# Reordering the first stage, the weight loads and the second product's first units of a fused attention and snake kernel

## The chip, the cores and the metric

The kernel runs on one core of a Trainium2 chip. The metric is the device time of one execution in microseconds (us). The kernel before takes 442.25 us (median of 3 runs, 441.99 to 442.3). The profile names these engines: TensorE (PE in the profile; its weight loads are PEld), VectorE (DVE), ScalarE (ACT), GpSimd (POOL), SyncE (SP, which only issues transfers) and the sixteen DMA engines. A profiled run gives a trace with the start of every instruction. Its span is a little shorter than the device time: 440.3 us in a run of 442.11. The record also has a mean granted TensorE clock for every run, profiled or not.

## The reference

Two things follow each other: attention with normalised q and k, then a two-layer product with the "snake" activation between the layers. Cut to what matters:

```python
# q, k, v: (8 batches, 12 heads, 448 tokens, 64)
rmsnorm = lambda x, g: x / np.sqrt(np.mean(x * x, -1, keepdims=True) + 1e-6) * g
scores = rmsnorm(q, g_q) @ rmsnorm(k, g_k).transpose(0, 1, 3, 2) / 8
attn = softmax(scores) @ v                       # softmax over the last axis
x = attn.transpose(0, 2, 1, 3).reshape(3584, 768)
h = x @ w_in                                     # w_in: 768 x 2048
g = h + np.sin(alpha * h) ** 2 / (alpha + 1e-9)  # snake
out = g @ w_out                                  # w_out: 2048 x 768
```

## The kernel before

The kernel works batch by batch. The first product of batch b is called h(b); the second product is called out(b) here. After h(b) TensorE works on out(b) and on the attention of batch b+1, mixed by a fixed plan, until h(b+1). The stage before h(0) has only attention in it: that is the first stage.

Heads come in pairs, and two head pairs are a *chunk* of q and k: chunks 0, 1 and 2 are batch 0, chunks 3, 4 and 5 batch 1, and so on. What the prediction calls the fifth chunk is chunk 4. Each chunk goes through seven steps: squares of q and of k, q times g, two reduces, root and scaling, transposition.

```python
st.steps = (lambda: square(0), lambda: square(1), fold_g, lambda: reduce(0), lambda: reduce(1),
            lambda: (rsqrt(), scale(0), scale(1)),
            lambda: (transpose(), load_qk(ci + 3) if ci + 3 < NC * B else None))
# transpose(): two DMA transposes on SyncE's queue; load_qk: q and k of a later chunk, on the same queue
# chunks 0 to 2 are transposed by TensorE instead, and VectorE scales them
```

The beginning of the first stage, and its end:

```python
BUSY = (20, 8)                                 # dummy products that keep TensorE busy
c0.square(1), c0.square(0)                     # ScalarE
c0.reduce(1), c0.reduce(0)                     # VectorE
c0.rsqrt(slice(1, 2)), c0.rsqrt(slice(0, 1))   # ScalarE: the two roots
keep_busy(BUSY[0], blank)
spread_g()          # GpSimd g_q*g_k, TensorE spreads it over the partitions, ScalarE copies it
keep_busy(BUSY[1], blank)
c0.fold_g()         # GpSimd: q times g
...
S_(), S_(), S_()    # a score tile (TensorE) and its exponential (ScalarE); S_(n): n dummies in it
c1.rsqrt()
S_(3)
c2.square(0), c2.square(1)     # ScalarE
...
S_()
v_parts[2](), v_parts[3]()
load_w_out(1)                  # second half of w_out, GpSimd's queue
A_(), A_()                     # values of the last two pairs, each 28 matmuls
step_of(NC + 1, 5, 6)()        # chunk 4: scaling (GpSimd), transposes, load of chunk 7
first_product(0, beside_h(0))
```

Out(0) was made in six units of 16 matmuls, each with its own eviction (VectorE copies PSUM to a buffer, which is stored from there).

## Time and profile before

| what | before |
|---|---|
| device time, median (range) | 442.25 us (441.99 to 442.3) |
| TensorE busy | 425.9 us, 97% of the span |
| first exponential / h(0) starts | 14.60 / 44.41 us |
| h(0) to h(1), and each later stretch | 50.36 us |
| half clock | 14.69 to 28.34 us |
| end of ScalarE's last work for h(0) (the last sine and its square), after the start of h's last matmul | 64.55 us, 2.15 us after |

The table is read from the timelines of TensorE and ScalarE. A program with TensorE 97% busy can only get shorter where TensorE waits or runs slowly, and both happen only in the first 95 us. The prediction shows the waits, chain and clock for it. Two more lines will be needed later. One is the issue of chunk 4's transposes in SyncE's timeline (start us, us, engine and line, operation, how many), and the other the end of ScalarE's work for h(0): the table load for the exponentials, which follows the last sine and its square ("the last sine" from here on).

```profile
51.11 14.27 SPq L254 DMA_TRANSPOSE qkT<-qkn  x2
```

```profile
64.57 1.28 ACT L504 ACT_TABLE_LOAD   x1
```

The transposes that were issued from 51.11 us on landed at 70.48 and 71.31 us (read, like all landings of transposes here, from the last semaphore increment of each in the trace). TensorE did not wait for them, since it was not there earlier.

### The profile page before, as it was taken

The numbers are of one execution on the slowest core, as the hardware profiler recorded it, in microseconds if no ns is written. First come the engines' busy times: TensorE is split into PE (matmuls) and PEld (weight loads), VectorE is DVE, ScalarE is ACT, GpSimd is POOL, SyncE is SP. The second block draws the span as 40 slices with busy tenths as digits, with TensorE's granted clock in tenths as the row PEclk, the third lists the DMA queues.
The fourth block names the chain that finished last, engine by engine and source line by source line (L and its number), as shares of the span: only waits on it lengthen the run. The fifth ranks groups of instructions, "written<-read, shape, count | busy, mean of one in ns | idle before, by whom it ended". The sixth has DMA issues, their size and how long they took to land.

```text
span 440.3 us, 9454 instructions
## 1 busy us (share of the span) xinstructions
PE 425.9 (97%) x3811; PEld 220.4 (50%) x3811; DVE 228.1 (52%) x331; ACT 340.1 (77%) x531; POOL 278.0 (63%) x262
## 2 busy tenths in 40 slices
PE   7788999899999999999999999999999999999996
PEld 3234544455555554555555555555555555555563
DVE  3576573456544564464645464545645474246611
ACT  4879888878888788887878788887878788788600
POOL 3867978937698287947599196965599285002300
PEclk9679999999999999999999999999999999999999
DMA  7899999592066803596064902598054900420022
GB/s 251 179 237 251 196 220 226 140 227 78 2 197 180 189 2 76 151 221 120 2 198 146 222 2 51 151 207 159 2 162 116 124 0 18 97 56 1 1 71 73
DMA packets 69296, 55.09 MB, mean 125 GB/s; under 512 B 41460, under 2 KB 65796, under 8 KB 69252
## 3 DMA queue, kind: packets, MB, share of 16 engines
q1 hardware_dynamic: 56690, 40.97, 37.2%
q0 software_dynamic: 11616, 11.81, 17.2%
q10 hardware_dynamic: 946, 1.70, 1.0%
q8 instruction: 30, 0.49, 0.5%
q14 instruction: 14, 0.11, 0.1%
HBM read 45.62 MB, written 11.01 MB: 129 GB/s over the span
## 4 chain that ended last, share of the span: by engine, by line
PE 85%; ACT 4%; POOL 3%; issue 2%; DVE 2%; DMA 2%; SPq 0%; POOLq 0%; DVEq 0%
PE hps L344 33%; PE ops L389 32%; PE av L308 12%; PE sc L292 8%; ACT expT L295 3%; POOL sq L220 2%; DMA g_rows<-in_g_q_dram 1%; POOL qk L223 1%; DMA out_dram<-osb 1%; DVE qkn L245 1%; POOL qkn L245 1%; DVE ms L226 0%; ACT rec L311 0%; PE tp L267 0%; DVE g_sb L331 0%
## 5 line engine op out<-in xcount | busy, mean ns | idle before, releaser
L295 ACT ACTIVATE expT<-sc 128x896 bf16<-128x896 f32 x168 | 145.0, 913 | 33.5 <-PE sc L292 32.2
L389 PE MATMUL ops<-w_out_sb,g_sb 128*128 128x384 bf16 x896 | 156.8, 327 | 0.8 <-DVE osb L395 0.7
L344 PE MATMUL hps<-xT,w_in_sb 128*128 128x448 bf16 x768 | 146.7, 353 | 0.0
L326 POOL TENSOR_TENSOR s<-s 128x448 f32<-128x448 f32 x64 | 59.2, 930 | 101.8 <-ACT s L323 91.0
L389 PEld LDWEIGHTS <-g_sb 128*128 128x128 bf16 x896 | 83.1, 98 | 70.9 <-issue 19.5
L331 DVE SCALAR_TENSOR_TENSOR g_sb<-s,inv_alpha_sb,hps 128x448 bf16<-128x448 f32 x128 | 80.7, 678 | 63.1 <-POOL s L326 63.1
L344 PEld LDWEIGHTS <-w_in_sb 128*128 128x128 bf16 x768 | 74.5, 98 | 71.5 <-issue 2.9
L323 ACT ACTIVATE s<-hps,alpha_sb 128x448 f32<-128x448 f32 x128 | 74.5, 627 | 28.0 <-PE hps L344 26.2
L245 POOL TENSOR_TENSOR qkn<-qk,inv 128x448 bf16<-128x448 f32 x84 | 76.1, 937 | 21.8 <-ACT inv L236 21.3
L317 DVE TENSOR_TENSOR xT<-av,rec 64x448 bf16<-64x448 f32 x96 | 59.7, 622 | 52.9 <-ACT rec L312 33.8
L220 POOL TENSOR_TENSOR sq<-qk 128x896 f32<-128x896 f32 x42 | 69.9, 1678 | 6.1 <-DVE ms L226 4.7
L308 PE MATMUL av<-expT,vb 64*64 64x448 bf16 x672 | 70.4, 353 | 1.2 <-ACT expT L295 1.1
L308 PE MATMUL av<-expT,ones 64*64 64x448 bf16 x672 | 70.4, 353 | 0.0
L226 DVE TENSOR_REDUCE ms<-sq 128x14 f32<-128x896 f32 x42 | 45.3, 1083 | 27.5 <-POOL sq L220 27.2
L292 PE MATMUL sc<-qkT 64*64 64x448 bf16 x672 | 52.1, 369 | 2.7 <-DVE qkT L274 1.1
L395 DVE COPY osb<-ops 128x768 f32<-128x768 f32 (+1 forms) x35 | 27.9, 797 | 50.0 <-PE ops L389 44.1
L223 POOL TENSOR_TENSOR qk<-qk,gg 128x896 f32<-128x896 f32 x24 | 50.1, 2088 | 4.9 <-ACT gg L171 3.3
L308 PEld LDWEIGHTS <-vb 64*64 64x64 bf16 x672 | 37.8, 108 | 15.4 <-issue 3.3
L308 PEld LDWEIGHTS <-ones 64*64 64x64 bf16 x672 | 37.3, 108 | 10.8
L328 ACT ACTIVATE s<-s 128x448 f32<-128x448 f32 x64 | 36.9, 577 | 2.9
L292 PEld LDWEIGHTS <-qkT 64*64 64x64 bf16 x672 | 15.1, 106 | 30.6 <-issue 25.8
L311 ACT ACTIVATE rec<-av 128x448 f32<-128x448 f32 x48 | 26.2, 546 | 3.6 <-PE av L308 3.1
(43 smaller groups left out, 138.9 us busy)
## 6 DMA issues: line engine op xcount, KB each, us to landing
qk<-in_q_dram SPq DMA_DIRECT2D x24, 448.0 KB, 4.9
qk<-in_k_dram SPq DMA_DIRECT2D x22, 448.0 KB, 5.4
out_dram<-osb SPq DMA_DIRECT2D x39, 192.0 KB, 2.9
vb<-in_v_dram POOLq DMA_DIRECT2D x32, 168.0 KB, 6.6
w_in_sb<-in_moe_w_in_dram POOLq DMA_DIRECT2D x2, 1536.0 KB, 20.0
w_out_sb<-in_moe_w_out_dram POOLq DMA_DIRECT2D x2, 1536.0 KB, 27.5
out_dram<-osb SPq DMA_DIRECT2D x26, 96.0 KB, 5.8
qk<-in_k_dram ACTq DMA_DIRECT2D x2, 448.0 KB, 6.0
```

The source lines that it names most:

```text
L220: nc.gpsimd.tensor_mul(st.sq[w], qk[ci][:, w], qk[ci][:, w])
L223: eng.tensor_mul(qk[ci][:, 0], qk[ci][:, 0], gg.to_broadcast([P, 2 * NJ, D]))
L245: eng.tensor_mul(n[:, :, hi, :], x[:, hi], inv[:, hi].unsqueeze(2).to_broadcast([P, NJ, D]))
L292: nc.tensor.matmul(sc[key_rows(pp, hi), pp, :S], qkt[r, 1, j * REST:(j + 1) * REST], qkt[r, 0, :], start=True, stop=True)
L295: nc.scalar.activation(expT[c, j], sc[:, :, :S], ACT.Exp, scale=SCALE)
L308: nc.tensor.matmul(av[o, part, :S], ones[r, :] if part else vb[b][r, hp, j, :], expT[pi // 2, j][r, pi % 2, :], start=(j == 0), stop=(j == ...
L317: nc.vector.tensor_mul(xT[b][r, hp, :], av[r, 0, :S], rec[o, :])
L323: nc.scalar.activation(s1, hps, ACT.Sin, scale=alpha_sb[:, m, :])
L326: nc.gpsimd.tensor_mul(s2, s1, s1)
L331: nc.vector.scalar_tensor_tensor(g_sb[:, m, (b % 2) * S:(b % 2 + 1) * S], s2, inv_alpha_sb[:, m, :], hps, op0=ALU.mult, op1=ALU.add)
L344: nc.tensor.matmul(ps[:, m % 2, :S], w_in_sb[:, kt, m * P:(m + 1) * P], x[:, kt, :], start=(kt == 0), stop=(kt == KT - 1))
L389: nc.tensor.matmul(st["ps"][:, k, :HALF], lhsT, w_out_sb[:, m, half * HALF:(half + 1) * HALF], start=(m == 0), stop=(m == MT - 1))
```

## The change

Its intent is to start the exponentials sooner, to take work off ScalarE's path, to bring w_in in halves so that it does not compete with chunk 4's q and k, to move chunk 4's scaling from before h(0) to beside it, and to evict out(0) in fewer, larger units. The core of it, cut:

```diff
-    BUSY = (20, 8)
+    BUSY = (11, 15)
...
-    w_in_sb = wpool.tile([P, KT, D_FF], BF16)
+    w_in_sb = [wpool.tile([P, KT, D_FF // 2], BF16, name=f"w_in_{half}") for half in range(2)]
...
         def square(w):
-            if early:
+            if ci < 2:                         # chunk 2's squares go to GpSimd
...
-        if m % 2 == 0:
+        if m % 2 == 0 and (b or m <= MT // 2): # three squares of h(0) go to ScalarE
             nc.gpsimd.tensor_mul(s2, s1, s1)
...
-        units = [(i, (0, 1)) for i in order] if b else [(i, (h,)) for h in range(2) for i in order]
+        units = [[(i, half) for half in range(2)] for i in order]
+        if b == 0:                             # four units of out(0): 32, 16, 32 and 16 matmuls
+            units = [[(i, half) for i in rows_] for half in range(2) for rows_ in (order[:2], order[2:])]
...
-    c0.rsqrt(slice(1, 2)), c0.rsqrt(slice(0, 1))
     keep_busy(BUSY[0], blank)
     spread_g()
+    c0.rsqrt(slice(1, 2)), c0.rsqrt(slice(0, 1))
     keep_busy(BUSY[1], blank)
...
-    S_(), S_(), S_()
+    S_(), S_()
     c1.rsqrt()
     S_(3)
-    c2.square(0), c2.square(1)
...
-    S_(2), S_(1), S_()
+    S_(3), S_(2), S_(2), S_(1)
...
+    nc.gpsimd.tensor_copy(gate, qk[NC + 1][:, 1, 0, 0:1])   # wait for chunk 4's k
+    load_w_in(1)
+    load_w_out(0)
...
+    load_w_out(1)
...
-    A_(), A_()
-    step_of(NC + 1, 5, 6)()
-    first_product(0, beside_h(0))
+    S_(), A_(2)            # the last two pairs together, their last tile last
+    c4.rsqrt()
+    beside = beside_h(0)
+    for i, task in ((2, c4.fold_g), (4, lambda: c4.scale(0)), (5, lambda: c4.scale(1)), (6, step_of(NC + 1, 6))):
+        beside.setdefault(i, []).append(task)
+    first_product(0, beside)
```

In every stretch between two h's, the one after h(0) included, three reduces of later chunks also come one slot of the plan later, and beside every h one product of q with g moves to the middle. The two roots of chunk 0 no longer share their PSUM banks. No experiment takes these small moves back alone.

## The prediction

> **What bounds the kernel now.** I read the summary first (TensorE busy 97% of the span), then the start times of the first product h of each of the eight batches, TensorE's waits, the chain in order of time up to 45 us, and the rows of ScalarE, GpSimd and VectorE in that stretch. In TensorE's timeline the h of the eight batches start at 44.41, 94.77, 145.12, 195.48, 245.83, 296.18, 346.54 and 396.89 us: from the first on, one batch every 50.36 us. The waits of TensorE after 40 us are only these (columns: waiting line, releaser, us in total, times, longest):
>
> ```profile
> PE av L308 <- ACT expT L295: 1.1, 2, 0.7
> PE sc L292 <- DVE osb L395: 1.0, 1, 1.0
> PE ops L389 <- DVE osb L395: 0.7, 1, 0.7
> ```
>
> So there is nothing to gain after the second h, and the first 44.4 us plus the stretch from h(0) to h(1) are all that the change can move. In the first stage the chain, in order of time, is (start, us, what):
>
> ```profile
> 1.28 4.28 DMA g_rows<-in_g_q_dram
> ...
> 9.61 2.09 POOL qk L223
> 11.70 0.02 issue
> 11.72 1.16 DVE qkn L245 x2
> ...
> 12.93 0.49 PE tp L267 x14
> ...
> 14.60 2.54 ACT expT L295 x3
> ...
> 42.77 1.71 PE av L308 x32
> 44.48 18.28 PE hps L344 x96
> ```
>
> The reader sees a latency chain up to the first exponential at 14.60 us: g arrives, GpSimd multiplies q by g (9.61 to 11.70), VectorE scales, TensorE transposes. From there ScalarE's program order rules, until the values of the last pair. ScalarE's rows (start, busy us, row, idle before) show what it spends and where it waits:
>
> ```profile
> 9.33 0.21 ACT L171 COPY gg<-gps 128x64 f32<-128x64 f32 x1
> ...
> 18.39 1.78 ACT L217 ACTIVATE g_sb<-qk 128x896 f32<-128x896 f32 x2
> 20.07 2.52 ACT L295 ACTIVATE expT<-sc 128x896 bf16<-128x896 f32 x3
> 24.34 0.92 ACT L295 ACTIVATE expT<-sc 128x896 bf16<-128x896 f32 x1 [1.74 <-PE sc L292]
> ...
> 28.80 0.54 ACT L311 ACTIVATE rec<-av 128x448 f32<-128x448 f32 x1 [0.99 <-PE av L308]
> ```
>
> From the first exponential (14.60) to the end of the last (42.72) are 28.1 us: 21 exponentials at 0.83 (three take 2.54) 17.4, four reciprocal pairs at 1.06 (28.80 to 29.86) 4.2, three pairs for the norm at 0.57 (17.01 to 17.58) 1.7, two squares 1.8, together 25.1; the other 3.0 us are waits. Last, the clock (columns end with granted clock, DMA share, GB/s):
>
> ```profile
> 4.40:14.70 10.30, 7.07 (x65) 3.55 (x63) 5.60 (x11) 5.67 (x12) 5.39 (x6) 1.00 0.69 221
> 14.70:28.30 13.60, 11.80 (x94) 4.30 (x92) 7.49 (x11) 11.00 (x16) 11.99 (x12) 0.50 1.07 236
> 28.30:44.40 16.10, 14.26 (x227) 6.80 (x219) 11.90 (x18) 14.70 (x23) 9.97 (x10) 1.00 1.12 247
> ```
>
> TensorE runs at half clock from 14.7 to 28.3 us, and the DMA engines are full from about 14 us on.
>
> **What the Trainium skill says.** "TensorE: Matmul & The Clock Gate", Part 1 (the HAM clock gate): TensorE's clock has two states, half and full, set by how busy it was in free-running windows of about 3.4 us. The trace agrees: 1.00 or 0.50, nothing between, and 13.6 us at half is four such windows. That is what the dummy products are for. The same page (engine queue depths) calls the queues of ScalarE, VectorE and GpSimd strict FIFO; the trace agrees where the eviction of out(0) at 73.82 us comes right after a reduce that began at 72.82 and had waited 2.62 us for GpSimd's square, while TensorE waited. "DMA: Bandwidth & Descriptors", SWDGE vs HWDGE vs iDMA: inside a DMA engine the queues are served in turn. The trace agrees: from 28 to 36 us GpSimd's queue (weights) moved 350 packets and SyncE's (q, k) 347; so each small packet of q, k waits for a large one of the weights, and that load took 11.7 and 13.7 us to land against medians of 4.9 and 5.4 over all such loads of this kernel.
>
> **The change part by part.**
> 1. *g ahead of the norm's root.* Now 20 dummies hold TensorE until 7.28 us and ScalarE's copy of g sits behind both roots (9.33). GpSimd's product of g is ready at 6.32. With 11 dummies (20 take 6.08 us, the early ones slower than the later, so 11 are done near 5) the small product runs from 6.35 to 6.8, and the copy fits behind the two squares (they end at 7.56) and ahead of the first root, which waits for VectorE's reduce until 7.88 anyhow. So q times g runs 7.85 to 9.94 instead of 9.61 to 11.70. The k scaling no longer waits for the second root (own bank): 8.85 to 10.0. The q scaling follows at 10.0 to 11.2. q, k of chunks 1 and 2 have landed by then (the last such landing is at 10.2), so the gates don't bind. The first exponential moves from 14.60 to about 12.9: 1.7 us.
> 2. *Squares of chunk 2 to GpSimd.* ScalarE loses 1.78 us, all on its path. GpSimd gains 2 x 1.68 = 3.3 us, and has it: its squares run about 16.3 to 19.6, and VectorE reduces them only after chunk 1's transposes.
> 3. *More dummies inside the first scores* (11 in place of 6 before chunk 1's transposes). At full clock these are 0.24 us each (8 in 1.90 at 7.57 us) and beside ScalarE; at half clock 0.48 (3 in 1.44 at 15.57), and the five score tiles with 11 dummies then take some 7 us against 5 x 0.83 of ScalarE. I expect the half-clock stretch to shrink, not to go. Walking ScalarE's order: two exponentials to 14.6, norm pair to 15.4 (reduces end at 14.75), five exponentials to 19.5, then chunk 1's transposes. At half clock these end near 19.95 and the next exponential starts 1.87 later (as now from 22.47 to 24.34), at 21.8: a wait of 2.3 us; at full clock 0.8. Three exponentials and the norm to 25.2, the first values' reciprocal 26.1 to 27.2 (wait 0.9 as now), four exponentials to 30.5, reciprocal to 31.7, three exponentials to 34.2, reciprocal and norm to 35.8, two to 37.5, reciprocal to 38.5, two to 40.15. Check by sum: 12.9 + 17.4 + 4.2 + 1.7 + waits of about 4 = 40.2.
> 4. *The last two pairs together, last tile last.* Now a whole pair of values (28 matmuls, about 1.3 us) stands between the last exponential and h; it ends at 42.72, h starts at 44.41. After: 24 matmuls of the second pair wait for the last exponential but one, then 8 (0.4 us) for the last one. About 0.85 in place of 1.7. h(0) then starts at 41.0: **3.4 us** earlier. The sixth k-tile of h is needed 3.8 us after its start, the last xT comes 3.2 after it by two reciprocals and four multiplies: no wait.
> 5. *Weights.* The same bytes, in halves of w_in. First half triggered at about 15, needed at 41; second at about 28, behind chunk 4's q, k, needed at 50 (9.1 us into h); w_out's first half after it, needed at 59; its second half at about 43.5, needed when the third unit starts, near 70. In the kernel before it was triggered at 45.6 and landed at 70.4; I expect 64 to 67.
> 6. *Chunk 4's scaling beside h.* 3.6 us of GpSimd and two transposes move from before h to about 16 us after its start. Three squares of GpSimd inside h go to ScalarE (0.58 each), which had idled 0.5 us per pair there: nearly free. The transposed chunk is needed at the eighth score tile, about 28.5 us after h's start, and is issued at 19: 9.5 us in hand, where the slowest such landing now took 13.5 and one on idle DMA engines 3.1.
> 7. *Units of out(0).* Four units of 32 and 16 matmuls in place of six of 16. The stretch h(0) to h(1) has 16 matmuls (2.6 us) fewer than a later one, yet takes the same 50.36: it holds 1.7 us of the waits shown and some 0.9 of smaller gaps. Fewer evictions stand between TensorE and a free bank; I count **1.8 us** of the 2.6.
>
> Sum: 3.4 + 1.8 = 5.2; 442.25 - 5.2 = 437.0.
>
> **The rivals.** *Transfers take the place.* Full DMA engines may not deliver w_out's second half or chunk 4's transposes in time now that TensorE comes 3.4 us earlier; my margins are 3 to 6 us and, with a landing of some 7 us, 2 to 3. For it: DMA share 1.0 and over up to 70 us, w_out landed at 70.4. Against it: first transfers start 1.7 earlier, and q, k of chunk 4 get ahead of the weights. It would give 438.5 to 440. *The clock.* If the added dummies keep full clock, chunk 1's wait falls by 1.5 us and the first values by 1: 434.5 to 435.5. If they only lengthen TensorE's share at half clock, ScalarE waits for scores: 438 to 439. *Nothing gained in out(0)*, because VectorE's eviction still stands behind a reduce waiting for GpSimd: 438.8.
>
> **Range and chances.** The two gains are bounded by 44.4 us of first stage, of which 23.3 is ScalarE's floor behind a start at 12.9, and by 2.6 us of out(0); all of it would be 8.5 us, just short of 2% (8.85). A loss needs a new wait of over 5 us. So within 2% is nearly sure; 435.0 to 440.0 holds the rivals.
>
> **What would show it.** First exponential near 12.9; h(0) near 41 and h(1) about 48.5 after it; no row of squares between the early exponentials; fewer than four half-clock windows or as many; no TensorE wait on a DMA. Wrong would be: the first exponential still past 14, TensorE waiting in the second half of h(0) or at the third unit for weights, or for the fifth chunk's scores, or 50.3 us again from h(0) to h(1).

## The result

| | before | after | said |
|---|---|---|---|
| device time, median of 4 fast runs | 442.12 (441.99 to 442.3) | 438.91 (437.79 to 440.08) | 437.0 |
| first exponential | 14.60 | 12.71 | 12.9 |
| end of last exponential, then h(0) | 42.72, 44.41 | 38.49, 39.56 | 40.15, 41.0 |
| h(0) to h(1) | 50.36 | 53.16 | 48.5 |
| h(1) to h(7) | 302.12 | 302.12 | no change |

All runs told of in this document are in the fast state. Ratios here are the mean time of one kernel's fast runs over that of the other's fast runs in the same rounds, so they are not quite the ratio of the medians quoted beside them. The ratio is 0.9927, with a 95% interval of 0.9901 to 0.9954. The kernel is 3.2 us faster, which counts as the same at 2%. The time is inside the predicted range, but 1.9 us above the point.

The two stretches went in opposite directions. The first stage got 4.85 us shorter, more than the 3.4 predicted. The stretch after it got 2.80 us *longer*, where 1.8 us less was predicted. Together that is 2.05 us, and the spans of the two profiled runs differ by just that (440.3 and 438.3). The profiled run of the changed kernel was its slowest one (440.08).

**The first stage after.** ScalarE's timeline (start, busy, row, idle before it and its releaser):

```profile
7.45 0.19 ACT L171 COPY gg<-gps 128x64 f32<-128x64 f32 x1
...
12.71 1.73 ACT L297 ACTIVATE expT<-sc 128x896 bf16<-128x896 f32 x2 [0.45 <-PE sc L294]
...
20.04 2.53 ACT L297 ACTIVATE expT<-sc 128x896 bf16<-128x896 f32 x3 [0.85 <-PE sc L294]
...
28.95 0.54 ACT L320 ACTIVATE rec<-av 128x448 f32<-128x448 f32 x1 [0.39 <-PE av L314]
```

The copy of g is 1.9 us earlier and so is the first exponential. The wait behind chunk 1's transposes is 0.85 us in place of 1.74. There is no row of squares among the exponentials. From the first to the end of the last exponential ScalarE needs 25.8 us in place of 28.1. The windows say why the waits shrank (columns end with granted clock, DMA share, GB/s):

```profile
14.70:28.30 13.60, 11.14 (x159) 5.29 (x164) 9.97 (x16) 11.61 (x18) 11.95 (x9) 1.00 1.09 237
28.30:39.50 11.20, 10.26 (x163) 4.90 (x151) 7.12 (x10) 9.61 (x17) 8.80 (x11) 1.00 0.95 208
```

The clock is 1.00 where the kernel before had 0.50. At the end of the stage, the chain of work shows the joined values of the last two pairs and h(0) right behind:

```profile
37.73 1.90 PE av L314 x36
39.62 4.28 PE hps L353 x22
```

Only 1.07 us lie between the end of the last exponential and h(0), where 1.69 did.

**From h(0) to h(1) after.** TensorE's waits from 38 to 100 us (us in total, times, longest):

```profile
PE sc L294 <- DMA qkT<-qkn: 1.8, 2, 1.4
PE sc L294 <- ACT expT L297: 1.0, 1, 1.0
PE av L314 <- DVE osb L406: 0.9, 1, 0.9
PE av L314 <- ACT expT L297: 0.7, 1, 0.7
PE sc L294 <- DVE g_sb L340: 0.3, 1, 0.3
```

The fourth of these lies before h(0). The other four add up to 4.0 us. The stretch without any wait would be 47.76 us (50.36 less the 16 matmuls it lacks, 2.6 us), so 53.16 has 5.4 us too much: 4.0 of listed waits and 1.4 of smaller gaps. The kernel before had 1.7 and 0.9. TensorE's timeline shows where the two new kinds of wait are:

```profile
63.88 0.38 PE L294 MATMUL sc<-qkT 64*64 64x448 bf16 x4 [1.03 <-ACT expT L297]
...
70.18 0.38 PE L294 MATMUL sc<-qkT 64*64 64x448 bf16 x2 [0.37 <-DMA qkT<-qkn]
71.97 0.76 PE L294 MATMUL sc<-qkT 64*64 64x448 bf16 x10 [1.41 <-DMA qkT<-qkn]
```

The scores of chunk 4 wait for its transposes. Where they come from is in SyncE's timeline:

```profile
48.86 0.79 SPq L122 DMA_DIRECT2D qk<-in_k_dram  x1
58.84 5.48 SPq L256 DMA_TRANSPOSE qkT<-qkn  x2
```

The chain of work has the second of them (start, us, what):

```profile
60.17 11.75 DMA qkT<-qkn
```

They were issued at 58.84 and 60.17 us, behind chunk 6's q and k in the same queue, and landed at 70.13 and 71.92 us. They were issued 7.7 and 1.2 us later than in the kernel before and landed within 0.6 us of the same moments. What changed is that TensorE now gets there earlier. From 64 to 68 us the DMA engines serve two queues (packets, MB, share of 16 engines): q0 is GpSimd's with w_out's second half, q1 SyncE's with the transposes.

```profile
q0 software_dynamic: 742, 0.57, 90.4%
q1 hardware_dynamic: 745, 0.19, 36.1%
```

Packet for packet they take turns, and each turn of w_out carries 768 bytes against 256 of the transposes. This is the round-robin of the Trainium skill ("DMA: Bandwidth & Descriptors", SWDGE vs HWDGE vs iDMA); the same page ("Queues, rings and completion order") says that within one queue's ring descriptors are consumed in order, which agrees with the packets of SyncE's queue in the trace: 1792 bytes each (q and k of chunk 6) up to 63 us, 256 bytes (the transposes) from then on.

One more landing belongs here. W_out's second half landed at 71.35 us, between the two transposes (70.38 in the kernel before).

The wait on the exponential comes from ScalarE being late at the end of h(0) (ScalarE's timeline):

```profile
52.73 0.63 ACT L332 ACTIVATE s<-hps,alpha_sb 128x448 f32<-128x448 f32 x1 [0.98 <-POOL s L335]
...
61.62 1.28 ACT L530 ACT_TABLE_LOAD   x1
```

The last sine ends 4.06 us after h's last matmul starts (61.60 and 57.54); before, 2.15 us. Sines wait for a buffer that GpSimd has not finished squaring, since GpSimd does chunk 4 in between: the wait of 0.98 us comes after chunk 4's q times g, and chunk 4's scaling follows at 55.19 us (GpSimd's timeline; the first line is the gate in front of w_in's second half):

```profile
30.68 0.18 POOL L501 COPY gate<-qk 128x1 f32<-128x1 f32 x1 [4.03 <-DMA qk<-in_k_dram]
...
49.72 2.09 POOL L224 TENSOR_TENSOR qk<-qk,gg 128x896 f32<-128x896 f32 x1
...
55.19 3.63 POOL L246 TENSOR_TENSOR qkn<-qk,inv 128x448 bf16<-128x448 f32 x4
```

The last wait, of 0.9 us, is for an eviction behind two reduces (VectorE's timeline):

```profile
79.36 2.08 DVE L227 TENSOR_REDUCE ms<-sq 128x14 f32<-128x896 f32 x2
81.47 0.96 DVE L406 COPY osb<-ops 128x768 f32<-128x768 f32 x1
```

### The profile page after: what moved, and what is told of

The parts are those of the page before. It is cut to its first block, busy times and chain, and to the rows that moved or that the text cites. A ratio compares the mean times of both kernels' runs of the same rounds, so it can differ in the third digit from the quotient of the medians.

```text
span 438.3 us, 9452 instructions
## 1 busy us (share of the span) xinstructions
PE 423.9 (97%) x3817; PEld 220.3 (50%) x3819; DVE 227.5 (52%) x329; ACT 340.0 (78%) x532; POOL 280.5 (64%) x264
## 4 chain that ended last, share of the span: by engine, by line
PE 83%; ACT 4%; DMA 4%; POOL 4%; DVE 2%; issue 2%; POOLq 0%; ACTq 0%
PE ops L400 31%; PE hps L353 30%; PE av L314 13%; PE sc L294 8%; DMA qkT<-qkn 3%; POOL qk L224 2%; ACT expT L297 2%; ACT s L332 1%; DMA qk<-in_k_dram 1%; POOL sq L221 1%; DVE ms L227 1%; DVE xT L326 1%; ACT s L337 1%; POOL vb L135 1%; DVE qkn L246 0%
## 5 line engine op out<-in xcount | busy, mean ns | idle before, releaser
L353 PE MATMUL hps<-xT,w_in 128*128 128x448 bf16 x768 | 146.7, 353 | 0.0
L335 POOL TENSOR_TENSOR s<-s 128x448 f32<-128x448 f32 x61 | 56.7, 934 | 114.6 <-ACT s L332 100.4
L353 PEld LDWEIGHTS <-w_in 128*128 128x128 bf16 x768 | 74.5, 98 | 71.5 <-issue 2.9
L221 POOL TENSOR_TENSOR sq<-qk 128x896 f32<-128x896 f32 x44 | 73.4, 1686 | 0.0
L314 PE MATMUL av<-expT,vb 64*64 64x448 bf16 x672 | 69.2, 349 | 1.8 <-ACT expT L297 0.9
L314 PE MATMUL av<-expT,ones 64*64 64x448 bf16 x672 | 69.2, 349 | 0.0
L227 DVE TENSOR_REDUCE ms<-sq 128x14 f32<-128x896 f32 x44 | 46.8, 1081 | 16.3 <-POOL sq L221 16.1
L337 ACT ACTIVATE s<-s 128x448 f32<-128x448 f32 x67 | 38.6, 577 | 3.5 <-DVE g_sb L340 0.5
L294 PEld LDWEIGHTS <-qkT 64*64 64x64 bf16 x672 | 15.3, 104 | 34.4 <-issue 28.5
```

Of the source, the lines that this page charges most:

```text
L221: nc.gpsimd.tensor_mul(st.sq[w], qk[ci][:, w], qk[ci][:, w])
L294: nc.tensor.matmul(sc[key_rows(pp, hi), pp, :S], qkt[r, 1, j * REST:(j + 1) * REST], qkt[r, 0, :], start=True, stop=True)
L314: nc.tensor.matmul(av[o, part, :S], ones[r, :] if part else vb[b][r, hp, j, :], expT[pi // 2, j][r, pi % 2, :], start=(j == 0), stop=(j == ...
L335: nc.gpsimd.tensor_mul(s2, s1, s1)
L353: nc.tensor.matmul(ps[:, m % 2, :S], w_in_sb[m * 2 // MT][:, kt, m % (MT // 2) * P:(m % (MT // 2) + 1) * P], x[:, kt, :], start=(kt == 0), ...
```

## The experiments

The theory after the first reading: the gain of the first stage was partly given back because chunk 4's transposes land at a time set by the DMA engines, because ScalarE is later at the end of h(0), and because one eviction stands behind reduces. The rivals: the added dummies decide the clock and so the first stage; the squares handed to ScalarE are what hurts; moving chunk 4's scaling was itself the mistake. Twelve kernels ran, in four sessions. In each the kernel before ran on the same chip, with medians of 442.17 to 442.42. The edits are against the changed kernel unless said otherwise. "h(0)" and "stretch" are the start of h(0) and the time from h(0) to h(1) in the one profiled run. All outputs were correct.

Two limits hold for all twelve. The changed kernel itself ran in none of these sessions; what it is compared with is its own four runs, all with a mean granted clock of 1.000. And the clock differs between runs of one kernel: in the profiles, a window of 3.41 us at half clock takes about 0.004 off the mean (0.996 in experiment 11 with one, 0.992 in experiment 4 with two), and profiles without one have 0.998 to 1.000. The slow warm-up before the first full clock is not in this mean.

### 1. Chunk 4 transposed by TensorE

```diff
-    ... (6, step_of(NC + 1, 6))):
+    ... (6, lambda: load_qk(NC + 4))):
...
+        if b == 1:
+            at[4].append(lambda: c4.pe_transpose((0, 1)))
```

> The changed kernel with one thing altered: the fifth chunk is transposed by TensorE (28 small matmuls and two VectorE copies, in the stretch after h(0)) and not by DMA. Theory A (its DMA transposes land too late, behind the second half of w_out; in the trace they land at 69.8 and 71.9 us and TensorE loses about 2.0 us to them): no wait on a DMA is left, TensorE pays 0.9 us for the transposes, h(0) to h(1) falls from 53.2 to about 52, the time from 438.9 to about 437.8. Rival B (ScalarE, behind after h(0), sets the pace and the DMA wait only stands in front of it): the wait turns into one on ScalarE's exponentials, h(0) to h(1) stays at 53 or rises by the 0.9, 438.9 to 439.8.

Measured: 440.05 us (438.81 to 440.29), ratio 0.9944 [0.9923, 0.9964]; h(0) at 40.93, stretch 52.21. The wait on the DMA is gone and the stretch is 0.95 us shorter, as far as TensorE's extra work and the remaining waits let it. The kernel is not faster. In its profile the front is 1.6 us late: the dummies ran at half speed, as TensorE's timeline shows, first of this kernel, then of the changed one.

```profile
7.01 5.17 PE L199 MATMUL ps<-blank 128*128 128x512 bf16 x15
```

```profile
6.39 3.41 PE L199 MATMUL ps<-blank 128*128 128x512 bf16 x15
```

The same fifteen dummies took 5.17 us in one run and 3.41 in the other. The Trainium skill ("TensorE: Matmul & The Clock Gate", Part 1) says that the windows of the clock gate are free-running and that the number of slow matmuls at the start differs from run to run; this agrees. It also says that the ramp costs under 1% of a typical span and should not be fitted. The 1.6 us here are 0.4% of the span, but they are half of what the whole change gains. On the time the experiment is inconclusive: what it saves in the stretch is lost in the front of this run, and its other three runs have no profile (mean clocks 0.999, 0.994 and 1.000).

### 2. The dummies inside the early scores taken back

```diff
-    S_(3)
+    S_()
     c1.scale(0), c1.scale(1)
     load_qk(NC)
-    S_(3), S_(2), S_(2), S_(1)
+    S_(3), S_(2), S_(1), S_()
```

> The changed kernel with the first chunk's scores again between 6 dummies and not 11 (order 0 0 0 3 2 1 0). Theory A (the added dummies keep the clock at full): half clock from about 15 us on for two to four windows, ScalarE waits 1.5 to 2.5 us more, h(0) starts at 41 to 42 in place of 39.6, time about 440.3. Rival B (the front's 15 dummies after g and the earlier scores suffice): granted clock 1.00, h(0) within 0.3 us of 39.6, time about 438.9.

Measured: 439.18 us (438.05 to 439.85), ratio 0.9930 [0.9909, 0.9950]; first exponential 12.92, h(0) at 39.76, full clock throughout this profile. So full clock is possible without the added inner dummies. That they do nothing for it is not shown: the other three runs have mean clocks of 0.995, 0.992 and 0.991, which is what one or two windows at half clock give, where all four runs of the changed kernel have 1.000. The stretch was 50.95 us in this profile, because the transposes happened to land at 68.82 and 69.66 (w_out at 68.70) and TensorE did not wait for them. That makes 2.2 us between this profile and the changed kernel's, with nothing edited there.

### 3. The units of out(0) as before

```diff
-            units = [[(i, half) for i in rows_] for half in range(2) for rows_ in (order[:2], order[2:])]
+            units = [[(i, half)] for half in range(2) for i in order]
```

> The changed kernel with out(0) again in six units of one row tile and one half. Theory A (the prediction's step 7: fewer evictions stand before a free bank): h(0) to h(1) 1 to 2 us longer, about 54.7, time about 440.4. Rival B (in this kernel other waits, on the late transposes and on ScalarE, hide what the units save): within 0.5 us, about 438.9.

Measured: 441.90 us (439.50 to 442.57, 20 runs), ratio 0.9986 [0.9976, 0.9995]; h(0) at 39.42, stretch 53.97. TensorE's waits now have the eviction on top:

```profile
PE sc L294 <- DVE osb L406: 2.2, 1, 2.2
```

From 0.9986 and 0.9927 the units are worth about 2.6 us of 442 in the changed kernel. Part of that is the clock: 14 of the 20 runs have means of 0.991 to 0.995. The six at 0.998 or more average 440.44 us, 1.5 over the changed kernel's 438.92, and the two profiled runs differ by 0.8. So the units are worth something between 0.8 and 2.6 us here.

### 4. The three squares of h(0) back on GpSimd

```diff
-        if m % 2 == 0 and (b or m <= MT // 2):
+        if m % 2 == 0:
```

> The changed kernel with the last three even squares of h(0) given back to GpSimd. Theory A (the three extra squares make ScalarE late after h(0): its first exponential there starts 5.4 us after h's last matmul, 3.5 in the kernel before): ScalarE is done 1 to 1.7 us sooner, time about 437.7. Rival B (GpSimd is full with the fifth chunk's scaling at that point, and ScalarE was late because its sine tiles wait for GpSimd): the last tiles of h(0) wait for GpSimd, which ends the scaling near 61 us only; time 440 to 442.

Measured: 440.19 us (439.36 to 441.94), ratio 0.9961 [0.9943, 0.9979]; h(0) at 41.15 with one window at half clock in the first stage (26.54 to 29.96 us) and a second one in the stretch (64.09 to 67.50), stretch 53.26. With the squares behind chunk 4's scaling, GpSimd does the last of them at 61.24 us, and TensorE waits once, longer than for anything else:

```profile
63.53 0.38 PE L294 MATMUL sc<-qkT 64*64 64x448 bf16 x4 [2.11 <-DVE g_sb L340]
```

By the ratios, handing them to ScalarE is worth about 1.5 us, though the two intervals overlap a little (0.9943 to 0.9954). The profile doesn't show that gain: its stretch is as long as the changed kernel's (53.16), the waits on the DMA and on ScalarE traded for this one, and its h(0) is 1.6 us late in a front where nothing was edited. The three runs at 0.998 or more average 439.69 us, 0.8 over the changed kernel. What is shown is that the squares on GpSimd are not better.

### 5. The front alone, on the kernel before

```diff
-    BUSY = (20, 8)
+    BUSY = (11, 15)
...
-    c0.rsqrt(slice(1, 2)), c0.rsqrt(slice(0, 1))
     keep_busy(BUSY[0], blank)
     spread_g()
+    c0.rsqrt(slice(1, 2)), c0.rsqrt(slice(0, 1))
```

> The kernel before with the front of the change alone: the copy of g ahead of the two roots, 11 and 15 dummies in place of 20 and 8 (one bank for both roots, as before). Theory A (the first exponential comes 1.7 us sooner and all after it follows): first exponential near 13.0 when the dummies find full clock, near 14.4 when they don't, h(0) at 42.5 to 43, time about 440.5 with a spread over runs of 1.5 us. Rival B (later waits in the first stage, on half clock and on values, take it back): h(0) at 44, time 442.

Measured: 441.31 us (440.73 to 442.01, 18 runs), ratio 0.9976 [0.9969, 0.9984]; first exponential 13.43, h(0) at 42.12, stretch 52.31. Half clock from 12.55 to 15.96 and 22.79 to 26.2 us. h(0) starts 2.3 us earlier, yet only 1.05 us stay: h(0) now stalls for 1.35 us on g_sb at 52.72, because GpSimd is scaling chunk 4 until 50.47 us and the squares of h wait for it. This is the reason for moving that scaling: an earlier front alone runs into it. Chunk 4's transposes land at 72.34 and 73.21 us here, and TensorE waits 0.5 us for them.

### 6. The units alone, on the kernel before

The edit is the whole change of the units (the `units` lines and the eviction and store that follow from them), on the kernel before:

```diff
-        units = [(i, (0, 1)) for i in order] if b else [(i, (h,)) for h in range(2) for i in order]
+        units = [[(i, half) for half in range(2)] for i in order]
+        if b == 0:
+            units = [[(i, half) for i in rows_] for half in range(2) for rows_ in (order[:2], order[2:])]
```

> The kernel before with the new units of out(0) alone. Theory A (the waits on evictions in that stretch go: 1.7 us, with the smaller gaps 2.6): h(0) stays at 44.4, h(0) to h(1) falls from 50.36 to 48 to 49, time about 440.5. Rival B (VectorE's eviction still stands behind a reduce that waits for GpSimd): 50 or more, time 442.

Measured: 441.32 us (440.90 to 442.29), ratio 0.9982 [0.9972, 0.9992]; h(0) at 44.19, stretch 49.39. Alone they gain 0.97 us of stretch and 0.8 us of time; in the changed kernel 0.8 to 2.6 (experiment 3). The same part may be worth more where TensorE arrives earlier, which is not shown. A reason that no run separates would be that the eviction is bound to a reduce that waits for GpSimd and does not move along.

### 7. Chunk 4's scaling ahead of h(0) again

```diff
-    for i, task in ((2, c4.fold_g), (4, lambda: c4.scale(0)), (5, lambda: c4.scale(1)), (6, step_of(NC + 1, 6))):
-        beside.setdefault(i, []).append(task)
+    c4.fold_g(), c4.scale(0), c4.scale(1)
+    step_of(NC + 1, 6)()
```

> The changed kernel with the fifth chunk's g, scaling and transposes issued before h(0), not beside it. Theory A (chunk 4's scaling beside h is what makes ScalarE late, as its sine tiles wait for GpSimd, and the transposes late): no wait on a DMA; ScalarE's last sine ends under 3 us after h's last matmul in place of 4.1; h(0) to h(1) falls to 49.5 to 50.5, time about 436.5. Rival B (GpSimd then starts the squares of h 3 us later and h(0) itself stalls for banks, or its first transposes are held up): h(0) to h(1) at 51 or more, time 438.5 to 440.

Measured: 441.03 us (440.12 to 442.46, 17 runs), ratio 0.9975 [0.9967, 0.9982]; h(0) at 39.55, stretch 54.13. There is no wait on the DMA, but h(0) itself stalls:

```profile
51.44 4.87 PE L353 MATMUL hps<-xT,w_in 128*128 128x448 bf16 x16 [2.64 <-DVE g_sb L340]
```

Half clock follows from 52.47 to 55.89 us. So moving the scaling beside h was right, by about 2.1 us from the ratios, although it made the transposes' issue later.

### 8. Eight dummies behind g in place of fifteen

```diff
-    BUSY = (11, 15)
+    BUSY = (11, 8)
```

> The changed kernel with 8 dummies after g and not 15. Theory A (at half clock the 15 dummies end at 12.1 us and hold up the transposes, as in the profile of the kernel with chunk 4 on TensorE, and this is much of the spread of 2.3 us over runs): first exponential at 12.6 to 13.1 in every run, spread under 1.5 us, median about 438.3. Rival B (the 15 are needed to reach full clock): half clock for some windows, h(0) at 40.5 to 41.5, time about 440.

Measured: 438.75 us (437.90 to 440.31), ratio 0.9922 [0.9898, 0.9947]; first exponential 12.69, h(0) at 39.53, stretch 50.95, no wait on the DMA in this profile, full clock from its first grant on. The time is that of the changed kernel, and so is the spread of 2.4 us, so the seven dummies are not the cause of the spread, as I had held. They do cost something in one case. In this profile the eight dummies ran at half speed, full clock coming only at 10.24 us, much as in experiment 1 (10.61):

```profile
6.85 3.56 PE L199 MATMUL ps<-blank 128*128 128x512 bf16 x8
```

Yet the first exponential came at 12.69 us, where fifteen slow dummies gave 14.34. On the other side, two of these four runs have mean clocks of 0.995 and 0.992, and they are the two slow ones (439.34 and 440.31).

### 9. Chunk 4's scaling first in h(0), squares of its first half on ScalarE

```diff
-        if m % 2 == 0 and (b or m <= MT // 2):
+        if m % 2 == 0 and (b or m >= MT // 2):
...
-    for i, task in ((2, c4.fold_g), (4, lambda: c4.scale(0)), (5, lambda: c4.scale(1)), (6, step_of(NC + 1, 6))):
-        beside.setdefault(i, []).append(task)
+    beside[0] += [c4.fold_g, lambda: c4.scale(0), lambda: c4.scale(1), c4.transpose]
+    beside[6] = [lambda: load_qk(NC + 4)]
```

> The changed kernel with the fifth chunk's g, scaling and transposes first in GpSimd's queue inside h(0), and in exchange the squares of h's first half on ScalarE and those of its second half on GpSimd (the other way round in the change). Theory A (both losses after h(0), the late transposes and the late ScalarE, come from chunk 4's 5.7 us of GpSimd standing between h's squares): transposes issued near 48 to 50 in place of 59, no wait on a DMA in any run, ScalarE's last sine 1 to 1.7 us sooner after h; h(0) to h(1) near 49 to 49.5; time 436 to 436.5. Rival B (ScalarE, now with sines and squares of the first half, falls behind TensorE in h(0), or the earlier transposes slow the weights so that out(0) waits for them): 438 or more.

Measured: 438.52 us (437.44 to 440.70), ratio 0.9914 [0.9885, 0.9942]; h(0) at 39.72, stretch 51.46. Two readings are clear. ScalarE's lateness is gone: the last sine ends 2.3 us after h's last matmul starts, and the wait on the exponential is 0.2 us in place of 1.0. So the order of work inside h(0) made it: chunk 4's scaling on GpSimd and the extra squares on ScalarE both lay in the second half of h. This run moves both and does not separate them. The landing, however, did not move: the transposes are issued at 49.26 and 56.78 us, up to 9.6 us earlier, and land at 69.52 and 70.39. TensorE still waits (its timeline):

```profile
69.56 0.38 PE L294 MATMUL sc<-qkT 64*64 64x448 bf16 x2 [1.28 <-DMA qkT<-qkn]
70.43 0.75 PE L294 MATMUL sc<-qkT 64*64 64x448 bf16 x10 [0.49 <-DMA qkT<-qkn]
```

In time it is no different from the changed kernel.

### 10. Experiment 9, eight dummies and later reduces together

On top of the edits of 8 and 9:

```diff
-                               (14, step_of(n4, 3)), (15, step_of(n4, 4)), (17, step_of(n3, 6)), (18, step_of(n4, 5)),
+                               (18 if b == 1 else 14, step_of(n4, 3)), (18 if b == 1 else 15, step_of(n4, 4)),
+                               (17, step_of(n3, 6)), (20 if b == 1 else 18, step_of(n4, 5)),
```

> The previous one with 8 dummies after g in place of 15 and, in the stretch after h(0) only, the reduces of the fifth chunk to come moved behind the third eviction of out(0) (with their scaling two slots later). If the losses add: h(0) at 39.5 in every run, the wait on the eviction (0.9 to 1.1 us) gone, h(0) to h(1) near 48 to 48.5, time about 435 to 435.5, spread under 1.5 us. If one stands behind another: 436 to 438.

Measured: 437.90 us (437.07 to 438.31), ratio 0.9887 [0.9866, 0.9908]; h(0) at 42.16, stretch 48.71. Of TensorE's waits little is left (the first line lies before h(0)):

```profile
PE av L314 <- ACT expT L297: 0.9, 2, 0.7
PE av L314 <- DVE osb L406: 0.2, 1, 0.2
PE sc L294 <- ACT expT L297: 0.2, 1, 0.2
```

The stretch is within 1.0 us of the 47.76 without waits. But the front of this profile ran at half clock for two of its windows (granted clock third from the end):

```profile
11.30:18.20 6.90, 6.86 (x40) 2.22 (x40) 5.17 (x10) 4.95 (x8) 6.88 (x9) 0.51 1.03 219
```

So h(0) came 2.6 us later than in the changed kernel, and that later arrival is also part of why nobody waited for the transposes. It has the lowest median of all, 4.5 us below the kernel before in its session, and is likely faster than the changed kernel too (all four runs have at least one window at half clock, with means of 0.990 to 0.996): the two intervals of the ratio overlap only between 0.9901 and 0.9908.

### 11. Later reduces alone (with eight dummies)

The edit is the one shown in experiment 10, with `BUSY = (11, 8)`, and nothing of experiment 9.

> The changed kernel with 8 dummies and the later reduces alone (chunk 4's scaling as in the change). Theory A (VectorE's queue makes the eviction wait behind two reduces and TensorE with it, 0.9 us in the trace): the wait of the values on the eviction goes, time 0.7 to 1.0 us under that of the kernel with 8 dummies, about 437.8. Rival B (TensorE meets ScalarE's lateness there instead, and the later scaling delays the transposes): no change or slower.

Measured: 439.07 us (438.51 to 439.51), ratio 0.9920 [0.9903, 0.9936]; h(0) at 40.80 with half clock from 13.03 to 16.45 us, stretch 50.28. The wait behind the reduces falls from 0.9 to 0.2 us, and the wait of 1.0 on the exponential stays. The time is that of experiment 8: the 0.7 us are visible in the trace, not in four or five runs, and all five here have means of 0.992 to 0.996.

### 12. Chunk 4's transposes ahead of chunk 6's q and k

Squares, scaling and reduces as in experiment 10, fifteen dummies, and:

```diff
-    step_of(NC, 5, 6)()
+    step_of(NC, 5)()
+    norm[NC].transpose()                      # without the load of chunk 6 behind it
...
+    beside[0] += [c4.fold_g, lambda: c4.scale(0), lambda: c4.scale(1), c4.transpose, lambda: load_qk(NC + 3)]
+    beside[6] = [lambda: load_qk(NC + 4)]
```

> The kernel with chunk 4's scaling first in h(0) and the later reduces, with 15 dummies again, and the load of chunk 6's q, k moved behind chunk 4's transposes in SyncE's queue. In all runs so far these transposes, issued from 49 to 60 us, landed at 68.4 to 71.9, because the queue serves them after chunk 6's q, k (which landed at 60 to 64) and packet for packet with w_out. Theory A (their place in SyncE's queue sets the landing): they land by 66 us, no wait of TensorE on a DMA, h(0) near 39.6 at full clock, h(0) to h(1) 48.5 to 49, time 435 to 436. Rival B (the landing is set by the end of w_out, whatever stands before): they land at 69 to 71 again, TensorE waits 1 to 2 us, time 437 to 438. Rival C (chunk 6's later q, k hold up GpSimd's squares and with them VectorE's evictions): no wait on chunk 4, but new ones near 75 us, time 437 or more.

Measured: 439.87 us (438.07 to 440.46), ratio 0.9929 [0.9914, 0.9945]; h(0) at 39.79, stretch 53.32. The transposes' packets now come before chunk 6's. They are issued at 49.25 and 52.59 us and land at 63.37 and 68.08, where experiment 9 had 69.52 and 70.39, and no score of chunk 4 waits for them: the place in the queue does move their landing. W_out's second half lands at 69.56, as in experiment 9 (69.69), so its end doesn't fix that landing whatever stands in the queue. But chunk 6's q and k land at 69.87 and 71.01 us (61.60 and 63.92 in the changed kernel), its squares start at 69.94 after a wait of 3.27 us, and the wait turns up one stage further (TensorE's waits):

```profile
PE sc L294 <- ACT expT L297: 2.5, 2, 2.3
...
PE ops L400 <- DMA w_out_sb<-in_moe_w_out_dram: 0.6, 1, 0.6
```

ScalarE's root of chunk 6 stood 3.16 us for VectorE's reduce at 74.41 us, and the exponentials stood behind it. Half clock from 75.88 to 79.29 us is in that profile as well. Experiment 10 kept the stretch at 48.71 us with the old order of the queue, if with a later h(0), so the swap did not pay in these runs.

## Why the prediction was right or wrong

**The time.** 438.91 us fell into the range, near its upper part; 5.2 us of gain were predicted and 3.2 came. The pieces erred in opposite directions: in the profiled runs the first stage gained 1.45 us more than said, and the stretch after it 4.6 less. That the sum stayed in the range is partly luck. The bound behind the range was also mis-added: 44.4 less 12.9, 23.3 and 0.85 is 7.35, with the 2.6 of out(0) 9.95, and not 8.5, so the prediction's own terms don't keep a gain below 2% (8.85).

**Step 1, g ahead of the root: right in size.** The first exponential came at 12.71 us, said 12.9. It is not as fixed as that: in experiment 1 the same front gave 14.34 us, because the fifteen dummies ran at half speed (eight slow ones left it at 12.69 in experiment 8).

**Step 2, squares of chunk 2: right.** 28.1 us from first to last exponential became 25.8, of which 1.78 are these squares.

**Step 3, "I expect the half-clock stretch to shrink, not to go": wrong.** It went, and with it 0.9 us of the wait behind chunk 1's transposes. The waits between the exponentials sum to 2.3 us where I had put about 4. This is the rival "the clock", though not by its cause: experiment 2 without the added inner dummies, and experiment 8 with the old eight behind g, both had full clock in their profiles, though not in all their runs. What does decide it is open. Experiments 10 and 11 (eight dummies behind g) and 5 (fifteen, on the kernel before) fell to half clock somewhere between 11 and 26.2 us, and all others of the new front with fifteen did not in that interval after warming up (experiment 4 did at 26.54). In experiments 10 and 11 full clock came early (4.52 and 6.21 us), the eight dummies were done in 1.90 us, TensorE then stood idle for 1.5 us, and half clock followed. With one profile each that is a hint, not a result.

**Step 4, last pairs together: right,** 0.62 us saved where 0.85 was said. Steps 2, 4 and 5 are read from the traces alone; no run takes them back one by one.

**Step 5, weights: sizes off, no wait.** The gate in front of w_in's second half waited 4.03 us for chunk 4's k; w_out's second half, triggered at 42.71, landed at 71.35 where 64 to 67 was expected. TensorE did not wait for either.

**Step 6 failed, in two terms.** Most of what the stretch lost against the predicted 1.8 us of gain is here. "The transposed chunk is needed ... about 28.5 us after h's start, and is issued at 19: 9.5 us in hand" gave a landing of some 7 us its place in the range. Need and issue were about right (19.3 us after h(0)), but the landing took 11.3 and 11.75 us. I took it as a duration that starts at the issue, and the 13.5 that I gave as the slowest was chunk 3's (the 3.1 "on idle DMA engines" had a DMA share of 0.76): chunk 4's own transposes already took 19.4 and 12.3 us in the kernel before, and the query that I read has no landing for them. It is a moment set by the bytes queued ahead and beside. In all twelve profiles with that queue order (the two kernels and experiments 2 to 11) the second transpose was issued between 56.8 and 62.7 us and landed between 69.3 and 73.2, each time 0.6 to 1.5 us after w_out's second half (68.0 to 72.3), which step 5 had at 64 to 67. Experiment 12 shows it from the other side, by moving the place in the queue. The second term, three squares to ScalarE "nearly free", is not refuted as a choice (experiment 4 is not faster), but was wrong in the cost. The sum left out that the sines then wait for GpSimd, which has chunk 4 between its squares: in the second half of h ScalarE waited 0.26 and 0.98 us for GpSimd and 0.48 for VectorE behind it, and ended 1.9 us later after h. TensorE lost 1.0 to 1.3 us by it, and the other order of experiment 9 takes that away.

**Step 7, units: mis-sized.** 1.8 us was said. They are worth 0.8 us alone (experiment 6) and 0.8 to 2.6 in the changed kernel (experiment 3). The reasoning "fewer evictions between TensorE and a free bank" holds; one eviction still stands behind two reduces and costs 0.9 us, which experiments 10 and 11 cut to 0.2.

**The rival that came true** is "transfers take the place", with its 438.5 to 440. It explains about 1.8 of the 5.4 us too many in the profiled run. The rest is ScalarE (1.3), the eviction (0.9) and smaller gaps (1.4).

**What stays open** is the spread. The kernel before stayed within 0.3 us in its four runs beside the changed one, and within 1.3 in 27 runs of another session; the changed kernel ranged over 2.3 us in four. Profiles of nearly the same kernel differ by 2.2 us in the stretch (53.16, and 50.95 in experiments 2 and 8) with whether the transposes land before they are needed, and by up to 1.6 us in the front with the clock. Either would make such a spread. The mean clocks of all runs tell part of it (us, and mean clock in brackets):

| kernel | its four runs |
|---|---|
| changed | 437.79 (1.000), 438.77 (1.000), 439.05 (1.000), 440.08 (1.000) |
| experiment 2 | 438.05 (0.998), 438.69 (0.995), 439.67 (0.992), 439.85 (0.991) |
| experiment 8 | 437.90 (1.000), 438.15 (1.000), 439.34 (0.995), 440.31 (0.992) |

In experiments 2 and 8 the time goes with the clock. In the changed kernel it doesn't. Its slowest run is the profiled one, which warmed up early (first exponential 12.71) and waited for the transposes, and the 2.3 us to its fastest run are about the 2.2 between a stretch of 53.16 and one of 50.95. So there the landing is the likely cause, which is not shown, as the other three have no profile. Experiment 10 with fifteen dummies was not run. If it kept its stretch with h(0) at 39.6, its time would be about 2.5 us lower, an estimate from the two profiles that supposes that the transposes still land in time. Experiment 9's waits speak against that.

## What to carry to other kernels

Where the DMA engines are full, do not count a transfer's time from its issue: add up the bytes ahead of it in its own queue and what the other queues take in turn, and read when the last needed one lands. Here that was just behind the end of the big transfer beside it. Making an engine arrive earlier at such a place, or swapping who comes first, only moved the wait in these runs. And when work moves beside a product, walk the order of the engine that receives it, since buffers that it frees late hold up a third engine.

## What the Trainium skill lacked or had wrong

- "DMA: Bandwidth & Descriptors" has both rules, ring order and round-robin by packets, but not what they make of a landing: the second transpose, issued between 56.8 and 62.7 us, landed between 69.3 and 73.2 us, 742 packets of 768 bytes taking turns with 745 of 256. No page has a time for a DMA transpose beside other traffic: 11.3 and 11.75 us in the changed kernel, 3.1 us in the kernel before for one issued at 123.44 us, with a DMA share of 0.76 meanwhile.
- "TensorE: Matmul & The Clock Gate", Part 1, advises against fitting the ramp, as it is under 1% of a span. Here it is 0.4%, yet the same 15 dummies took 3.41 or 5.17 us, as much as half the gain being measured. It would help to be told to compare several runs.
- The same part gives no measure of how busy a window must be. In the kernel before, half clock began at 14.69 us, after 3.41 us in which TensorE's records were busy for 1.50; in the changed kernel the clock stayed full through the 3.40 us from 21.5 with 2.37 busy, and in experiment 10 half clock lasted from 11.35 to 18.17 with 6.86 of 6.90 busy.
